# Column stretches of 512 instead of 384 in batches 1 to 3 of an attention and token mixer, with a new order of the work

## The chip, the cores and the metric

The kernel runs on one core of a Trainium2 chip. TensorE (PE) multiplies, with its weight loads shown apart as PEld; VectorE (DVE), ScalarE (ACT) and GpSimd (POOL) work element by element; SyncE (SP) issues the transfers. The metric is the device time of one execution in microseconds, the median of several runs. The runs of the kernel before have a median of 217.35 us and a lowest time of 216.99 us.

## The reference, cut to what matters

For 4 batches of 1088 tokens a linear attention is computed, four heads of 32 columns each, whose features are the 64 products of two 8-wide projections of a query or a key:

```python
a = einsum('rd,bhsd->bhsr', S1, x); b = einsum('rd,bhsd->bhsr', S2, x)
phi(x) = outer(a, b)                         # 64 features
x = (phi(q) @ (phi(k)^T v)) / (phi(q) @ sum(phi(k)) + 1e-6)   # B x 1088 x 128
h = relu(x^T @ w_tok1) @ w_tok2              # over tokens, 256 wide
u = x + h^T
out = u + relu(u @ w_ch1) @ w_ch2            # over channels, 1536 wide
```

The weights arrive as 64-bit floats; the kernel rebuilds 32-bit floats from them with integer operations.

## The kernel before, in words

A plan of named operations is built, and a list of names, `ORDER` (line 67), says in which order they are issued. Every engine runs its own instructions in that order. A suffix such as `@pool` chooses the engine, and `~4` asks for four filler matmuls. The sets of buffers (`bufs`, line 223) set how far one engine can run ahead of another.

The names: `K1.p` projects the keys of batch 1, `K1.v0`, `v4`, `v8` form their products on DVE, `K1.s` sums them against the values on PE and `K1.kvz` copies the result; `Q1.p` projects queries, `Q1.w`, `Q1.r` write and read them back by DMA and `Q1.m` multiplies. `A1.x` is the attention itself, `A1.n`, `A1.r`, `A1.d` its division, `A1.h` and `A1.l` split the result in a rounded high part and the rest. `A1.t` and `A1.w` are the two token products; `A1.xb` transposes x on DVE, `A1.xm` and `A1.xT` carry it through DRAM, `A1.us` adds it, and `A1.uh`, `A1.ul` split the sum u. `w20.abs` to `w20.add` convert piece 0 of the third weight, `w20.hi` and `w20.lo` split it.

The channel product is cut along the tokens into stretches, `U0` to `U11` (lines 42 to 57). Batch 0 has stretches of 384, 384 and 320 columns. Batches 1 to 3 are laid end to end, and their 3264 columns are cut into seven stretches of 384, one of 320 and one of 256, so that a stretch may hold the end of one batch and the start of the next. For each of the 12 pieces of the 1536 channels of a stretch there are four operations: `U.f`, three matmuls into a bank of `ps_h` (line 928); `U.h`, the rectified high part on ACT (line 932); `U.l`, the rest on DVE (line 935); and `U.s`, three matmuls that add into the bank of `ps_o` that collects the stretch's output (line 941). A high part and its rest stay in one of `HID` = 4 sets until `U.s` has read them. At a stretch's end `U.ol` adds the output to u on DVE (lines 960, 966) and `U.out` stores it (line 977). There are 3 banks of `ps_h`, 2 of `ps_o` and 3 of `ps_a`; `K0.s` sums into a bank of `ps_o`, `K1.s` to `K3.s` into one of `ps_a` (line 477).

The loads are issued by SP in the order of `LOADS` (line 36) for batches 0 and 1 and the weights, and where `ORDER` names them for batches 2 and 3.

Of the kernel before, what the change touches and what calls it, by code (L numbers as in the profile page):

```python
# [10 lines left out]
F32R = mybir.dt.float32r  # L11
# [49 lines left out]
HID = 4  # L61
# [9 lines left out]
v0 ~2 K0.s00 K0.s04 Q0.a10 K0.v8 K0.s08 Q0.m10 w01.shift w01.merge d04 d03 Q0.a11 Q0.b11 Q0.m11 w04.abs
w04.clamp@dve w03.abs w03.clamp@dve Q0.p2 Q0.a20 Q0.m20 Q0.a21 Q0.b21 w03.shift w04.shift d13 d10 Q0.m21 w03.merge
d12 K0.s10 K0.s14 K0.s18 w01.add d11 d20 K0.kvz ~2 A0.x0 w03.low q1 A0.n0 w10.abs A0.x1 A0.n1 k1 w04.merge A0.r0
A0.d0 d30 w04.low w04.add A0.r1 d31 w10.clamp@dve A0.d1 A0.x2 A0.t0 A0.n2 A0.t1 A0.r2 w03.add w10.shift A0.d2 Q1.p
w12.abs w11.abs w12.low v1 w20.abs w10.merge w12.clamp@dve w11.clamp@dve d21 d15 w10.low Q1.c0 w10.add Q1.c1 w11.low
# [10 lines left out]
w14.merge w15.low U0.h U0.s w15.add U0.h U0.l w01.hi U0.l U0.f w00.hi U0.h U0.l w02.hi U0.f U1.f w14.add w00.lo@dve
U0.h w10.hi U0.s A0.w2 U1.h U1.l U0.s K1.kvz A0.uh22 U0.l U1.f w15.hi U0.oh@pool U1.h U0.s Q1.r0None Q1.r00 Q1.r01
Q1.r1None Q1.r10 Q1.r11 Q1.m00@dve Q1.m11@pool U0.s U1.s U1.f U1.h Q1.m01@pool U1.f U1.l w03.lo@pool U1.s U1.oh@pool
w13.hi U1.f U0.ol Q1.m10@dve U0.out A0.ul22 w13.lo@pool w02.lo@pool A1.x w01.lo@pool U1.l U1.h U1.l w14.hi q2
w10.lo@pool U1.f U1.h U1.l U1.s U1.s w04.lo@pool U1.s A1.n0 U2.f U2.f k2 v2 A1.r0 A1.d0 q3 A1.n2 A1.r2 U1.h A1.n1  # L90
# [30 lines left out]
U9.s U9.h U10.f U9.l U10.f U9.l U10.h U9.s U10.f U10.h U9.s U10.h U9.s U10.l U10.l U10.s U10.f U10.f U10.s U9.ol
U9.out U10.h U10.h U10.l U10.s U10.l U10.f U10.f U10.s U10.h U10.h U10.l U10.f U10.s U10.h U10.l U10.s U10.f U10.h
U10.l U10.f U10.s U10.h U10.l U10.f U10.h U10.l U10.l U10.f U10.s U10.l U11.f U10.s U10.s U10.h U10.l U11.f U10.s
U11.f U11.h U11.h U11.h U11.l U11.l U10.s U11.s U11.f U11.f U11.s U10.ol U10.out U11.l U11.h U11.h U11.f U11.h U11.s
# [928 lines left out]
```

## Time and profile before

| what | value |
|---|---|
| median of the runs | 217.35 us |
| lowest run | 216.99 us |
| the profiled execution, its own time | 216.37 us |
| its span, first to last instruction | 213.9 us |
| PE busy | 209.5 us, 98% |
| PEld busy | 199.1 us, 93% |
| DVE busy | 147.1 us, 69% |
| ACT busy | 116.2 us, 54% |
| POOL busy | 60.9 us, 28% |
| DMA, mean over the span | 133 GB/s |

Busy time of PE overstates its use, since matmuls overlap and their ends are modelled. The chain of waits, which counts each stretch of time once, gives what a matmul really costs in a stream: the time of a piece divided by its matmuls. A timeline row gives the start, the length, the engine, the line and the shapes of one group of instructions.

### The profile page before, as it was taken

The numbers are of one execution on the slowest core, as the hardware profiler recorded it, in microseconds if no ns is written. First come the engines' busy times: TensorE is split into PE (matmuls) and PEld (weight loads), VectorE is DVE, ScalarE is ACT, GpSimd is POOL, SyncE is SP. The second block draws the span as 40 slices with busy tenths as digits, with TensorE's granted clock in tenths as the row PEclk, the third lists the DMA queues.
The fourth block names the chain that finished last, engine by engine and source line by source line (L and its number), as shares of the span: only waits on it lengthen the run. The fifth ranks groups of instructions, "written<-read, shape, count | busy, mean of one in ns | idle before, by whom it ended". The sixth has DMA issues, their size and how long they took to land.

```text
span 213.9 us, 4865 instructions
## 1 busy us (share of the span) xinstructions
PE 209.5 (98%) x1876; PEld 199.1 (93%) x1876; DVE 147.1 (69%) x299; ACT 116.2 (54%) x282; POOL 60.9 (28%) x66
## 2 busy tenths in 40 slices
PE   8999999999999999999999999999999999999993
PEld 7779779999998999999999999999999999999993
DVE  2899999998789765777434666585547656556562
ACT  4788997988456245444344544443336453544541
POOL 3177686989971001301000660010000010000000
PEclk9999999999999999999999999999999999999999
DMA  6999985750778598300697400014400200100000
GB/s 223 402 405 409 399 328 129 138 146 10 241 304 242 148 193 171 135 3 3 203 221 184 123 29 0 3 37 142 120 0 0 78 0 0 37 3 37 0 31 25
DMA packets 11398, 28.35 MB, mean 133 GB/s; under 512 B 1520, under 2 KB 5616, under 8 KB 11376
## 3 DMA queue, kind: packets, MB, share of 16 engines
q1 hardware_dynamic: 11232, 27.79, 41.7%
q8 instruction: 14, 0.23, 0.5%
q10 hardware_dynamic: 144, 0.26, 0.5%
q14 instruction: 8, 0.07, 0.1%
HBM read 23.21 MB, written 4.83 MB: 131 GB/s over the span
## 4 chain that ended last, share of the span: by engine, by line
PE 97%; ACT 1%; DVE 0%; issue 0%
PE ps_o L941 34%; PE ps_h L928 33%; PE ps_a L758 5%; PE ps_a L692 4%; PE ps_a L878 4%; PE ps_o L264 3%; PE ps_a L483 3%; PE ps_a L436 2%; PE ps_a L874 2%; PE ps_a L752 1%; PE ps_a L574 1%; PE ps_o L483 1%; PE ps_a L629 1%; PE ps_h L574 1%; PE ps_a L783 1%; PE ps_a L792 1%
## 5 line engine op out<-in xcount | busy, mean ns | idle before, releaser
L935 DVE SCALAR_TENSOR_TENSOR hl<-ps_h,hh 128x384 fp32r<-128x384 f32 (+2 forms) x144 | 74.5, 531 | 46.0 <-ACT hh L932 45.3
L932 ACT ACTIVATE hh<-ps_h 128x384 fp32r<-128x384 f32 (+2 forms) x144 | 67.4, 474 | 63.1 <-PE ps_h L928 54.0
L928 PE MATMUL ps_h<-uh,halves 128*128 128x384 f32 (+2 forms) x288 | 85.4, 330 | 0.0
L941 PE MATMUL ps_o<-hh,halves 128*128 128x384 f32 (+2 forms) x288 | 71.2, 330 | 0.0
L928 PEld LDWEIGHTS ps_h<-uh,halves 128*128 128x128 f32 x288 | 53.1, 188 | 0.6
L941 PEld LDWEIGHTS ps_o<-hh,halves 128*128 128x128 f32 x288 | 50.2, 188 | 0.8 <-issue 0.4
L928 PE MATMUL ps_h<-ul,halves 128*128 128x384 f32 (+2 forms) x144 | 47.1, 327 | 0.0
L941 PE MATMUL ps_o<-hl,halves 128*128 128x384 f32 (+2 forms) x144 | 47.1, 327 | 0.0
L852 POOL TENSOR_TENSOR ul<-us,uh 128x320 fp32r<-128x320 f32 (+4 forms) x10 | 7.2, 727 | 71.1 <-ACT uh L849 71.1
L928 PEld LDWEIGHTS ps_h<-ul,halves 128*128 128x128 f32 x144 | 27.1, 188 | 0.2 <-DVE ul L852 0.2
L941 PEld LDWEIGHTS ps_o<-hl,halves 128*128 128x128 f32 x144 | 27.1, 188 | 0.0
L307 POOL TENSOR_TENSOR whole<-c,tail 128x512 int32<-128x512 int32 (+3 forms) x11 | 11.7, 1072 | 2.7 <-ACT tail L290 1.3
L286 ACT ACTIVATE c<-doubles 128x512 f32<-128x512 f32 (+3 forms) x17 | 10.5, 625 | 3.1 <-DMA doubles<-wt 2.5
L466 DVE TENSOR_TENSOR k_p<-ps_a,a_sb 128x1024 f32<-128x1024 f32 (+1 forms) x12 | 11.0, 947 | 0.0
L722 POOL TENSOR_TENSOR xl<-x,xh 128x384 fp32r<-128x384 f32 x3 | 3.0, 1014 | 26.0 <-ACT xh L718 26.0
L290 ACT ACTIVATE tail<-doubles 128x512 int32<-128x512 uint32 (+3 forms) x17 | 10.4, 625 | 0.0
L300 DVE SCALAR_TENSOR_TENSOR c<-doubles,ps_h 128x512 int32<-128x512 int32 (+3 forms) x17 | 10.3, 609 | 0.2
L297 DVE TENSOR_SCALAR ps_h<-c 128x512 int32<-128x512 int32 (+3 forms) x17 | 10.2, 613 | 0.1
L758 PE MATMUL ps_a<-halves,xh 128*128 128x256 f32 x54 | 9.8, 283 | 0.0
L692 PEld LDWEIGHTS ps_a<-kvz,qp 128*64 128x64 f32 x288 | 8.7, 138 | 0.9 <-issue 0.7
L692 PE MATMUL ps_a<-kvz,qp 128*64 128x66 f32 x288 | 9.3, 223 | 0.0
L264 PE MATMUL ps_o<-still 128*128 128x128 f32 x38 | 8.0, 364 | 1.1 <-DVE still L242 1.1
(85 smaller groups left out, 238.7 us busy)
## 6 DMA issues: line engine op xcount, KB each, us to landing
qp<-rows SPq DMA_DIRECT2D x6, 544.0 KB, 5.0
br<-rows SPq DMA_DIRECT2D x12, 272.0 KB
doubles<-wc SPq DMA_DIRECT2D x6, 512.0 KB, 5.9
v_sb<-v SPq DMA_DIRECT2D x4, 594.0 KB, 10.6
doubles<-wt SPq DMA_DIRECT2D x4, 512.0 KB, 5.4
k_sb<-kT SPq DMA_DIRECT2D x3, 576.0 KB
xm<-xb SPq DMA_DIRECT2D x3, 576.0 KB
xT<-xm SPq DMA_DIRECT2D x12, 144.0 KB, 3.2
```

The costliest lines, as they stand in the source:

```text
L264: nc.tensor.matmul(spare_ps[:, :P], lhsT=still, rhs=still, start=True, stop=True)
L286: nc.scalar.activation(f32(t["c"]), f32(high), AF.Abs)
L290: nc.scalar.activation(t["tail"], low.bitcast(U32), AF.Copy, scale=2.0 ** -29)
L300: nc.vector.scalar_tensor_tensor(t["c"], high, -(1 << 30), t["ps"], op0=ALU.bitwise_and, op1=ALU.bitwise_or)
L307: engines[e].tensor_tensor(dst(), t["c"], t["tail"], op=ALU.add)
L466: engines["pool" if on_pool else "dve"].tensor_tensor(t["k_p"][:pn, t0 * H:t1 * H], a.unsqueeze(3).broadcast_to([pn, n, R, R]), t["sb", t0 ...
L692: nc.tensor.matmul(x_ps[c:c + 64, o:o + 2 * (D + 1)], lhsT=qp[:, p, s0 + c:s0 + c + 64], rhs=kvz_all[b % 2][:, p, :2 * (D + 1)], start=Tru ...
L758: nc.tensor.matmul(t["h_ps"][:, :DTOK], lhsT=t[l][:m, i, :], rhs=part(0, piece, r, j * DTOK, DTOK)[:m], start=(i == 0 and k == 0), stop=(i ...
L928: nc.tensor.matmul(h_ps[:, :cn], lhsT=part(2, at[2][e][0], l, at[2][e][1] * P, P), rhs=r[:, :cn], start=(m == 0), stop=(m == 2))
L932: nc.scalar.activation(t["hh"][:, :cn], t["h"][:, :cn], AF.Relu)
L935: nc.vector.scalar_tensor_tensor(t["hl"][:, :cn], t["h"][:, :cn], 0.0, f32(t["hh"][:, :cn]), op0=ALU.max, op1=ALU.subtract)
L941: nc.tensor.matmul(outs[i][:, :cn], lhsT=part(3, at[3][e][0], l, at[3][e][1] * P, P), rhs=r[:, :cn], start=(e == 0 and m == 0), stop=(e == ...
```

## The change: what it does

The stretches of batches 1 to 3 become five of 512 columns, one of 448 and one of 256, so that there are ten stretches, `U0` to `U9`, instead of twelve. The sets for the high part and its rest grow to 512 columns, and there are 3 instead of 4; those of u (`u`, `uh`, `ul`) go from 4 to 3. In the last stretch every fourth channel piece uses the buffers `xh` and `xl` of the attention result instead. `K2.s` and `K3.s` sum into a bank of `ps_o`. The loads of queries, keys and values of batches 2 and 3 are issued as two transfers of 64 partitions each, and so is the store of `U3`. `LOADS` and `ORDER` are written anew.

```diff
-LOADS = "00 q0a 02 k0 q0b 01 v0 04 03 13 10 12 11 20 q1 k1 30 31 v1 21 15 14 32 22".split()
-WIDE = 384
+LOADS = "00 q0a 02 k0 q0b 01 03 v0 04 10 12 20 11 13 q1 30 k1 31 21 v1 32 22 15 14".split()
+WIDE = 512
...
-    for n in (384,) * 7 + (320, 256):
+    for n in (512,) * 5 + (448, 256):
...
-HID = 4
+HID = 3
+HALVED = {"q2", "k2", "v2", "q3", "k3", "v3"}
 ORDER = """
...
+U3.s U4.f U4.h U4.h U3.ol U4.l U4.l U4.f U4.h A2.t2 U4.f U4.s U4.s U4.f U4.h A2.relu A2.hT A2.hTh U4.l U4.l U4.f
...
-    bufs = {..., "u": 4, "uh": 4, "ul": 4, ...
+    bufs = {..., "u": 3, "uh": 3, "ul": 3, ...
...
     def load(name, dst, src, nbytes, after=(), takes=(), uses=(), boost=0.0):
+        cuts = (0, P // 2, P) if name in HALVED else (0, P)
         def emit(_):
-            nc.sync.dma_start(dst(), src)
+            t = dst()
+            for p0, p1 in zip(cuts, cuts[1:]):
+                nc.sync.dma_start(t[p0:p1], src[p0:p1])
...
-                    t["kv"] = bank("ps_a" if b else "ps_o")
+                    t["kv"] = bank("ps_a" if b == 1 else "ps_o")
...
+                lent = i == len(SPANS) - 1 and e % 4 == 3
-                ps, hid = Hold("ps_h"), Hold("hid")
+                ps, hid = Hold("ps_h"), Hold("xs" if lent else "hid")
...
+                    if lent:
+                        t["hh"], t["hl"] = (new(x, [P, NT, P], F32R).rearrange("p t c -> p (t c)") for x in ("xh", "xl"))
...
+                    cuts = (0, P // 2, P) if i == 3 else (0, P)
+                        for p0, p1 in zip(cuts, cuts[1:]):
+                            nc.sync.dma_start(out[b][p0:p1, c0:c0 + m], outs["sb", i][p0:p1, d0:d0 + m])
```

Three places show how the order moves. The first is PE in the start, from the second query projection to the attention of batch 0. Rows with `still` are fillers, `s_spread` is `Q0.p`, `k_p` is `K0.s`, and `kvz` is `A0.x`. Before:

```order
L264 MATMUL ps_o<-still 128x128 x3
L574 MATMUL ps_a<-q_sb,s_spread 128x384 x2
L574 MATMUL ps_h<-q_sb,s_spread 128x384 x2
L264 MATMUL ps_o<-still 128x128 x2
L483 MATMUL ps_o<-v_sb,k_p 64x66 x18
L574 MATMUL ps_a<-q_sb,s_spread 128x320 x2
L574 MATMUL ps_h<-q_sb,s_spread 128x320 x2
L483 MATMUL ps_o<-v_sb,k_p 64x66 x18
L264 MATMUL ps_o<-still 128x128 x2
L692 MATMUL ps_a<-kvz_84,qp 64x66 x36
```

and now:

```order
L261 MATMUL ps_o<-still 128x128 x2
L575 MATMUL ps_a<-q_sb,s_spread 128x384 x2
L575 MATMUL ps_h<-q_sb,s_spread 128x384 x2
L261 MATMUL ps_o<-still 128x128 x4
L575 MATMUL ps_a<-q_sb,s_spread 128x320 x2
L575 MATMUL ps_h<-q_sb,s_spread 128x320 x2
L484 MATMUL ps_o<-v_sb,k_p 64x66 x36
L261 MATMUL ps_o<-still 128x128 x2
L693 MATMUL ps_a<-kvz_84,qp 64x66 x36
```

One filler fewer stands ahead of the second query projection and two more behind it, and the key sums stand behind the third projection in one piece.

The second place is DVE around the transposition of batch 2's attention result. `rec` and `x` are the division, `xb` the transposition, `xl` and `ul` splits, and `hl` is `U.l`. Before:

```order
L935 SCALAR_TENSOR_TENSOR hl<-ps_h,hh 128x384 x3
L704 RECIPROCAL rec<-den 128x12 x2
L712 TENSOR_TENSOR x<-ps_a,rec 128x384 x2
L704 RECIPROCAL rec<-den 128x12
L712 TENSOR_TENSOR x<-ps_a,rec 128x384
L812 STREAM_TRANSPOSE xb<-x 128x1152
L935 SCALAR_TENSOR_TENSOR hl<-ps_h,hh 128x384
```

and now:

```order
L940 SCALAR_TENSOR_TENSOR hl<-ps_h,hh 128x512
L723 TENSOR_TENSOR xl<-x,xh 128x384
L713 TENSOR_TENSOR x<-ps_a,rec 128x384
L853 TENSOR_TENSOR ul<-us,uh 128x256
L705 RECIPROCAL rec<-den 128x12
L713 TENSOR_TENSOR x<-ps_a,rec 128x384
L813 STREAM_TRANSPOSE xb<-x 128x1152
L940 SCALAR_TENSOR_TENSOR hl<-ps_h,hh 128x512
```

One division moved ahead of the `U.l` above it, and two splits came into the piece of the row that has no `U.l`.

The third place is PE around the key sums of batch 3, `K3.s`. `uh` rows are `U.f`, `hh` and `hl` rows `U.s`, `s_rows` is `Q3.p`. Before:

```order
L928 MATMUL ps_h<-uh,halves_500 128x384
L483 MATMUL ps_a<-v_sb,k_p 64x66 x36
L629 MATMUL ps_a<-q_sb,s_rows 32x272 x8
L941 MATMUL ps_o<-hh,halves_790 128x384 x2
L941 MATMUL ps_o<-hl,halves_790 128x384
```

and now:

```order
L946 MATMUL ps_o<-hh,halves_674 128x512 x2
L946 MATMUL ps_o<-hl,halves_674 128x512
L484 MATMUL ps_o<-v_sb,k_p 64x66 x36
L693 MATMUL ps_a<-kvz_84,qp 64x66 x36
L930 MATMUL ps_h<-uh,halves_653 128x512
```

The sums now go into a bank of `ps_o` in the middle of stretch `U3`, directly ahead of batch 2's attention; the next user of that pool, the first `U4.s`, takes the bank of `U3` and so comes behind `U3.ol`, as the line of `ORDER` in the diff has it.

## Rows read from the trace of the kernel before

**Rows 1.** The page's parts 1 and 2: busy time of each engine, and the span in 40 slices, the busy share of PE in tenths and the granted clock in tenths of full speed.

```profile
PE 209.5 (98%) x1876; PEld 199.1 (93%) x1876; DVE 147.1 (69%) x299; ACT 116.2 (54%) x282; POOL 60.9 (28%) x66
...
PE   8999999999999999999999999999999999999993
...
PEclk9999999999999999999999999999999999999999
```

**Rows 2.** The chain of waits in the start, in order of time: start us, length us, what.

```profile
11.12 0.65 PE ps_h L574 x4
11.77 0.64 PE ps_o L264 x4
12.41 1.20 PE ps_o L483 x36
13.61 0.74 PE ps_a L574 x4
14.35 0.54 PE ps_h L574 x4
14.89 1.20 PE ps_o L483 x36
16.09 0.64 PE ps_o L264 x4
16.73 2.25 PE ps_a L692 x72
18.98 2.79 PE ps_a L752 x12
21.77 0.73 PE ps_a L629 x16
...
24.38 0.44 PE ps_a L792 x2
```

**Rows 3.** The chain of waits later on, the same columns: pieces of 384, 320 and 256 columns, and the end.

```profile
179.11 2.08 PE ps_o L941 x12
...
193.34 0.88 PE ps_h L928 x6
...
206.03 1.06 PE ps_o L941 x9
...
209.21 1.43 PE ps_o L941 x12
210.63 0.02 issue
210.66 0.42 DVE o_sb L966
```

**Rows 4.** Groups of instructions by line and shape, on DVE: busy us and mean ns of one, then idle time before them.

```profile
L935 DVE SCALAR_TENSOR_TENSOR hl<-ps_h,hh 128x384 fp32r<-128x384 f32 x108 | 58.4, 553 | 37.2 <-ACT hh L932 36.5
...
L935 DVE SCALAR_TENSOR_TENSOR hl<-ps_h,hh 128x256 fp32r<-128x256 f32 x12 | 4.9, 424 | 3.1 <-ACT hh L932 3.1
...
L812 DVE STREAM_TRANSPOSE xb<-x 128x1152 f32<-128x1152 f32 x3 | 4.1, 1380 | 0.1
```

**Rows 5.** The same view on ACT.

```profile
L932 ACT ACTIVATE hh<-ps_h 128x384 fp32r<-128x384 f32 x108 | 52.4, 492 | 49.6 <-PE ps_h L928 43.0 <-PE ps_o L941 6.0
...
L932 ACT ACTIVATE hh<-ps_h 128x256 fp32r<-128x256 f32 x12 | 4.5, 383 | 4.4 <-PE ps_h L928 3.8 <-PE ps_o L941 0.6
```

**Rows 6.** Timeline of SP's issues: start us, length us; the first two are the issue of weight piece 20 and of `q1`, the others the first and last `Q1.r` and the store of `U0` with the four loads behind it.

```profile
10.52 0.33 SPq L268 DMA_DIRECT2D doubles<-wc  x1
12.03 0.33 SPq L268 DMA_DIRECT2D q_sb<-qT  x1
...
33.08 0.63 SPq L659 DMA_DIRECT2D qp<-rows  x1
...
35.78 1.28 SPq L662 DMA_DIRECT2D br<-rows  x2
53.93 0.36 SPq L977 DMA_DIRECT2D outT<-o_sb  x1
54.34 0.43 SPq L268 DMA_DIRECT2D q_sb<-qT  x1
```

**Rows 7.** The page's part 2 again, what the DMA moved in GB/s in each of the 40 slices, and from part 6 the reads of `Q.r`, KB each and us to landing.

```profile
GB/s 223 402 405 409 399 328 129 138 146 10 241 304 242 148 193 171 135 3 3 203 221 184 123 29 0 3 37 142 120 0 0 78 0 0 37 3 37 0 31 25
...
qp<-rows SPq DMA_DIRECT2D x6, 544.0 KB, 5.0
```

**Rows 8.** Timeline of POOL, the first two products `Q1.m`.

```profile
50.41 3.64 POOL L672 TENSOR_TENSOR qp<-qp,br 128x544 f32<-128x544 f32 x2
```

**Rows 9.** Timeline of DVE around the division and transposition of batch 2: start us, length us, what, and idle time before it.

```profile
95.45 1.08 DVE L935 SCALAR_TENSOR_TENSOR hl<-ps_h,hh 128x384 fp32r<-128x384 f32 x2 [0.19 <-ACT hh L932]
98.02 0.32 DVE L704 RECIPROCAL rec<-den 128x12 f32<-128x12 f32 x2 [1.49 <-ACT den L700]
98.38 1.02 DVE L712 TENSOR_TENSOR x<-ps_a,rec 128x384 f32<-128x384 f32 x2
...
100.16 1.38 DVE L812 STREAM_TRANSPOSE xb<-x 128x1152 f32<-128x1152 f32 x1
101.47 0.52 DVE L935 SCALAR_TENSOR_TENSOR hl<-ps_h,hh 128x384 fp32r<-128x384 f32 x1
```

More of the change, by code (lines that the diff above doesn't have):

```diff
@@ L71 @@
[L71 to L75, printed above, removed]
@@ L86 @@
[L86 to L90, printed above, removed]
@@ L121 @@
[L121 to L124, printed above, removed]
-U11.l U11.f U11.l U11.f U11.s U11.s U11.l U11.s U11.f U11.h U11.h U11.l U11.f U11.s U11.l U11.f U11.s U11.h U11.h
@@ L126 @@
-U11.l U11.l U11.f U11.s U11.h U11.h U11.s U11.l U11.l U11.s U11.s U11.ol U11.out
+s k0a d00 s.abs s.clamp s.shift s.merge s.low s.add ~4 K0.p0 s.rows q0a w00.abs w00.clamp@dve K0.c0 K0.v0 w00.low
+w00.shift d02 k0 Q0.s0@pool Q0.s1@pool ~1 Q0.p0 w02.abs Q0.a00 ~1 K0.p4 w02.clamp@dve Q0.b01 w00.merge w00.add
+Q0.m00 Q0.a01 Q0.m01 K0.c8 q0b ~2 Q0.p1 K0.c4 d01 w02.low w02.shift K0.v8 w02.merge w02.add w01.abs K0.v4 Q0.a10
+Q0.m10 w01.clamp@dve w01.shift Q0.b11 Q0.a11 Q0.m11 d03 w03.abs w01.low ~4 Q0.p2 v0 K0.s00 K0.s04 d04 w03.clamp@dve
@@ new lines @@
+Q0.a20 w01.merge w01.add w04.abs w04.clamp@dve Q0.m20 w04.low Q0.a21 Q0.b21 Q0.m21 d10 w10.abs K0.s08 K0.s10 K0.s14
+K0.s18 K0.kvz ~2 A0.x0 w03.shift w10.low A0.n0 w04.shift w03.merge w04.merge w04.add d12 w12.abs d20 d11
+w10.clamp@dve A0.r0 A0.d0 w12.clamp@dve A0.x1 A0.n1 A0.r1 d13 w10.shift A0.d1 A0.x2 A0.t0 A0.t1 w03.low w03.add q1
+w12.low A0.n2 A0.r2 w20.low w10.merge w10.add A0.d2 Q1.p w13.abs w11.abs w12.shift w11.clamp@dve w13.clamp@dve
+w20.abs w11.shift w20.clamp@dve w12.merge w11.merge w12.add Q1.c0 Q1.c1 d30 w13.low w11.low k1 A0.t2 w11.add
@@ new lines @@
+w20.shift A0.relu ~2 A0.hT K1.p d31 d21 w13.shift w20.merge w20.add v1 w30.abs d32 w30.clamp@dve Q1.w0 A0.hTh
+w13.merge w13.add d22 K1.c0 K1.v0 w30.shift w30.merge A0.u0 A0.w0 A0.u1 A0.w1 K1.c4 w30.low w02.hi K1.c8 w20.hi
+w20.lo@pool A0.uh00 A0.ul00 U0.f U0.f Q1.w3 w21.abs K1.v4 U0.f w31.abs K1.v8 d15 Q1.w1 w31.clamp@dve K1.s
+w21.clamp@dve A0.uh11 U0.h A0.ul11 w30.add w30.hi w30.lo@pool U0.h w22.abs w31.low U0.h w22.clamp@pool w21.low U0.l
+U0.l U0.s w21.shift U0.l w21.merge w21.add w31.shift w31.merge w31.add w32.abs w32.low w12.hi w32.clamp@dve U1.f
@@ new lines @@
+U1.h U0.s U1.f U1.h A0.u2 U0.s w21.hi w21.lo@pool w15.low U1.f U1.h d14 Q1.w2 w22.low q2 U1.l U1.l w31.hi U1.s
+w22.shift U1.l w31.lo@pool w22.merge U0.f U0.h w22.add K1.kvz U0.l U1.s U1.s U0.f U0.f U0.s U1.f w14.abs
+w14.clamp@dve U0.h w15.abs U0.h U0.l U0.l w15.clamp@pool U0.s U1.h U1.l U1.f U0.s w22.hi w32.shift U1.f U1.h U1.h
+w10.hi U1.l w32.merge w22.lo@pool U1.l w15.shift w15.merge w32.add U1.s U1.s U0.f U0.f w15.add w11.hi w14.low U0.h
+U0.l U0.h U1.s w32.hi w32.lo@pool U0.f U0.h U0.l U0.s U0.s w14.shift U0.l w14.merge U0.f Q1.r0None U0.f U0.f U0.h
@@ new lines @@
+U7.s U8.h U8.l U8.s U8.f U8.h U8.l U8.s U8.h U8.l U7.ol U8.f U8.h U8.l U8.f U8.f U8.h U8.l U8.s U8.h U8.s U8.f U8.l
+U8.h U8.l U8.s U8.f U8.h U8.f U8.f U8.l U8.s U8.h U8.s U8.s U8.h U8.l U8.f U8.f U8.h U8.s U8.l U8.l U8.s U8.s U8.h
+U8.l U9.f U9.h U9.l U9.f U8.s U9.h U9.l U9.f U9.h U9.f U9.h U8.ol U8.out U9.f U9.l U9.l U9.s U9.s U9.s U9.f U9.h
+U9.h U9.f U9.s U9.l U9.s U9.f U9.l U9.f U9.s U9.h U9.l U9.s U9.f U9.h U9.h U9.l U9.l U9.f U9.s U7.out U9.f U9.h U9.h
+U9.l U9.l U9.h U9.l U9.s U9.s U9.s U9.s U7.out U9.ol U9.out
@@ L266, in load @@
     def load(name, dst, src, nbytes, after=(), takes=(), uses=(), boost=0.0):
+        cuts = (0, P // 2, P) if name in HALVED else (0, P)
         def emit(_):
-            nc.sync.dma_start(dst(), src)
-        op = plan.add(name, {"sp": 475.0}, emit, (), takes, uses, boost, order=after)
+            t = dst()
+            for p0, p1 in zip(cuts, cuts[1:]):
+                nc.sync.dma_start(t[p0:p1], src[p0:p1])
+        op = plan.add(name, {"sp": 475.0 * (len(cuts) - 1)}, emit, (), takes, uses, boost, order=after)
         op.bytes, op.rate = nbytes, 395.0
@@ L498, in keys @@
         n = f"K{b}"
-        kp_hold, kv_hold = Hold("k_p"), Hold("ps_a" if b else "ps_o")
+        kp_hold, kv_hold = Hold("k_p"), Hold("ps_a" if b == 1 else "ps_o")
         sb = {i: Hold("a_sb") for i in (0, 4, 8)}
```

82 lines of the change are left out of this document (34 added, 48 removed).

## The prediction

> **What bounds the kernel now.** I read the page's shares first, then the chain of waits from the start to the end, then groups by shape, and last the issues of SP. PE is busy 98% of the span and in every slice but the first and the last, at full granted clock throughout [rows 1]. Busy time alone would not prove that PE is the bound, because overlapping matmuls are counted in full; the chain does. From 24.38 us, the transposes of batch 0's token product, the chain runs on PE without a break to the last matmul, whose piece ends 1.43 us after 209.21 [rows 2, 3], and the page's chain names no other engine there. What follows is one addition of 0.42 us and the last store. In the start the chain runs on PE too, but part of what it runs there is filler (two pieces of 0.64 us in [rows 2]).
>
> So three things can move the end: how long PE's own work takes after 24.38 us, when that point comes, and any wait that the new order puts into a stream that has none.
>
> What a matmul costs in the stream is read from the pieces of the chain. Twelve of 384 columns take 2.08 us, which is 173.3 ns each; six of 320 take 0.88 us, 146.7 ns each; nine of 256 take 1.06 us, 117.8 ns each [rows 3]. From 320 to 384 columns that is 26.6 ns for 64 columns, 0.416 ns a column, and what stays beside the columns is 173.3 - 384 x 0.4167 = 13.3 ns at 384, 13.3 ns at 320 and 11.1 ns at 256.
>
> **The change part by part.**
>
> *Wider stretches.* Each stretch has 12 x 6 = 72 matmuls whatever its width. Before, batches 1 to 3 take 7 x 72 at 173.3, 72 at 146.7 and 72 at 117.8 ns: 87.3 + 10.6 + 8.5 = 106.4 us. After, 5 x 72 = 360 are of 512 columns, 72 of 448 and 72 of 256. No row has 512 or 448 columns. With the fixed 13.3 ns a matmul of 512 takes 226.7 ns and one of 448 takes 200.0 ns: 81.6 + 14.4 + 8.5 = 104.5 us. That is **1.9 us less**, the fixed part of the 144 matmuls that disappear. The bounds: if the part beside the columns grows in proportion, 512 costs 173.3 x 512 / 384 = 231.1 ns and 448 costs 202.2, in all 106.2 us, and the gain is 0.2 us; if it is the smallest that the rows show, 11.1 ns, the sum is 360 x 224.4 + 72 x 197.8 + 72 x 117.8 = 103.5 us, and the gain is 2.9 us. I take 13.3 ns, because the two nearest widths, 384 and 320, both show it.
>
> [...]
>
> *DVE and ACT.* `U.l` costs 553 ns at 384 columns and 424 at 256 [rows 4], about 1.0 ns a column, so 682 ns at 512; `U.h` costs 492 and 383 [rows 5], so 600 ns at 512. A channel piece of 512 columns gives PE 6 x 226.7 = 1.36 us of work, so both keep up, with more room than now (553 of 1.04 us). Their saved fixed parts are worth nothing, since PE covers them.
>
> *The start.* Ahead of the second query projection one filler goes (two fillers, four rows of the trace, take 0.64 us, so 0.32), behind it two are added (0.64), and the key sums come in one piece behind the third projection [rows 2]. Counted on from the row at 16.73, the attention of batch 0 starts 0.3 us later, at 17.05, and with it all that hangs on it, to the point at 24.38. Is something else later? Weight piece 03 now goes ahead of `v0`. In the rows SP issues piece 20 at 10.52 and `q1` at 12.03 [rows 6], with gaps before them that I read as waits for the landing of the eighth transfer before; for `q1`, the sixteenth, that is `v0`, so `v0` lands at about 12.0. Piece 03 is 512 KB, at 402 to 409 GB/s [rows 7] 1.3 us, so `v0` lands at 13.3. PE reaches the key sums at 12.41 - 0.32 + 0.64 + 1.28 = 14.0. It is covered by 0.7 us. Behind it the weights of the first token product and `q1` have the same bytes ahead of them. I take **+0.3 us**; the bounds are 0 (if the fillers only fill a wait, as they are meant to) and +1.0 (if the 0.7 us of cover is gone and as much again is lost).
>
> *SP.* The halves add six issues of loads and one of a store, about 0.4 us each [rows 6], on a queue that stands idle for long. `q2` is now ahead of the `Q1.r` reads, 544 KB or about 1.4 us at the rate of [rows 7]. Those reads were issued from 33.08, the last pair over 1.28 us from 35.78, and take 5.0 us to land [rows 6, 7], so until about 42; their first products start at 50.41 [rows 8]. Eight microseconds cover the 1.4. The other loads of batch 2 no longer stand behind the store of `U0` at 53.93 [rows 6], which only makes them earlier. Nothing waits for either on PE, so I cost both at nothing. The new store order at the end leaves the last stretch at 256 columns with the same addition of 0.42 us, so the end costs what it did.
>
> *Banks and sets.* `K3.s` now takes one of two output banks inside stretch `U3`, so the first `U4.s` waits for `U3.ol`, an addition of 512 columns (about 0.7 us, like `U.l`) behind `U3`'s last `U.s`. The order puts two `U4.f`, the last third of `A2.t` and a third `U4.f` between: 3 x 0.68 + 9 x 117.8 ns = 3.1 us of PE work. Covered. Without that cover it would cost 0.7 us and the hand-overs. With three sets instead of four, the time that DVE may be late shrinks: a set is held for `U.h`, `U.l` and `U.s`, at 384 columns 0.49 + 0.55 + 0.52 = 1.56 us, and four sets give 4 x 1.04 = 4.16, so 2.6 us to spare; at 512 it is 0.60 + 0.68 + 0.68 = 1.96 of 3 x 1.36 = 4.08, so 2.1; at 384 with three sets 3.12 - 1.56 = 1.6. I cost this at 0, between a gain of 0 (no wait exists to remove) and the loss of the second rival.
>
> **The sum:** -1.9 + 0.3 = -1.6 us. The span goes from 213.9 to 212.3 us, the profiled execution from 216.37 to 214.8. The median of the runs is 217.35, 1.0 us above the profiled one; I predict the median, 217.35 - 1.6 = **215.8 us**.
>
> **The rivals.**
>
> 1. *No gain from width.* What stands beside the columns grows with them, as it does from 256 to 320 (11.1 to 13.3 ns), and 512 columns cost 231.1 ns. Then 217.35 - 0.2 + 0.3 = 217.5 us. Against it: 320 and 384 show the same 13.3 ns. [...] Chance 0.14 for both.
>
> 2. *Slower: DVE is late for `U.s`.* DVE has stretches without a `U.l` in each of batches 1 to 3. In the row before, `U.l` ends at 96.53 and the next starts at 101.47 [rows 9]; its own work there is three divisions and the transposition, 3 x 0.5 + 1.38 = 2.9 us. Where such a stretch is longer than the time to spare, PE stands still for the rest. With 2.1 us to spare that is 0.8 us for batches 2 and 3, with 1.6 in stretch `U1` 1.3 us for batch 1; the splits that now stand in batch 2's piece add about 1.0. In all 0.8 + 0.8 + 1.3 + 1.0 = 3.9 us, so 217.35 - 1.6 + 3.9 = 219.7 us. It decides the sign from 1.6 us of such waits on. Against it: in [rows 9] nearly 5 us pass without a `U.l` and the chain still has no break, because PE runs the attention, key sums and token products meanwhile, and the new order has them there too. Chance 0.20 for 217.9 to 221.7; over that, 0.05 more, which takes some of the same in the converting of the weights, where DVE has no idle time to lend.
>
> 3. *More gain.* The start is not later and the fixed part is 11.1 ns or the fillers yield: 217.35 - 2.9 = 214.4, and as much as 1 us below that if the first weights, now loaded in another order, let the point at 24.38 come earlier. For it: PE holds filler in the start. Against it: the key sums cannot start before their products, which the same DVE row delivers. Chance 0.11, of which 0.03 lies below 213.0.
>
> That the change would not do what it says can be left out: the order has the 512-column rows.
>
> **How the numbers follow.** The forecast has the remaining 0.50, from about 214.9 to 217.0, since waits of up to 1 us in a new order are likely somewhere. The range must hold 8 in 10: forecast, rival 1, rival 3 down to 213.9 and the lower part of rival 2 up to 218.6, together about 0.82. Two per cent of 217.35, about what a measurement of this kernel can tell from no change, is 4.3 us: faster means below 213.0 (0.03), slower above 221.7 (0.05), and the rest, 0.92, is within.
>
> **What would show it.** In the changed kernel's chain a `U.f` or `U.s` of three 512-column matmuls should take 0.68 us; 0.69 or more is rival 1. The transposes of batch 0 should start at 24.4 to 24.9. The chain from there on should name PE alone; pieces of DVE (`hl`) or ACT (`hh`) in it, and PE rows with idle time put down to them, are rival 2, first to be looked for behind `A1.x`, `A2.x` and `A3.x` and at the first `U4.s`. The forecast is wrong if the clock granted is not full throughout, or if PE waits for `v0`.

## The result and the profile after

On the same chip the changed kernel has a median of 218.35 us (216.13 to 220.41, 15 runs) and the kernel before one of 216.24 us. The ratio is 1.0066, with a 95% interval of 1.0036 to 1.0095: **0.7% slower**. That is within 2%, but of the other sign. 218.35 us lies inside the range, 2.5 us above the number I gave; but on this chip the kernel before took 1.1 us less than the 217.35 us that I had counted from, and the ratio put on 217.35 gives 218.8 us, just above the range. The comparisons leave disturbed runs out.

The page of the changed kernel, parts 1 and 2, answers to [rows 1] and [rows 7]; the DMA row is the busy share of the DMA engines in tenths, the last row GB/s.

```profile
span 216.8 us, 4522 instructions
PE 209.5 (97%) x1734; PEld 183.2 (84%) x1734; DVE 142.4 (66%) x267; ACT 112.0 (52%) x257; POOL 68.8 (32%) x71
PE   8998999999599999999999999999999999999994
PEclk9999999999799999999999999999999999999999
DMA  6999996998406699530697200034010010000020
GB/s 218 376 409 404 409 365 163 156 169 178 133 4 181 192 221 199 150 92 8 189 276 191 54 0 0 3 157 109 0 48 3 0 51 0 0 3 0 0 91 24
```

142 matmuls fewer, and PE as busy as before. One slice has a hole, the eleventh, 54.2 to 59.6 us; the clock is lower in the same slice; and in the three slices ahead of it the DMA engines are busy eight tenths of the time or more and move 156 to 178 GB/s. Neither the hole nor the lower clock is in [rows 1].

The chain of waits of the changed kernel, in the start, around the hole, and later (start us, length us, what):

```profile
16.96 1.72 PE ps_a L693 x53
18.68 0.57 issue
19.24 0.80 PE ps_a L693 x19
...
37.80 16.94 DMA br<-rows
...
54.86 0.20 DVE qp L673
...
55.82 1.52 DVE qp L673
...
57.38 3.58 PE ps_a L693 x68
...
160.34 2.06 PE ps_h L930 x9
...
200.24 1.80 PE ps_o L946 x9
...
212.44 1.37 PE ps_o L946 x12
...
213.84 0.42 DVE o_sb L971
```

A chain that ran on PE alone from 24.38 us on now leaves it: the matmuls of `A1.x` wait for a product `Q1.m` on DVE, and that waits for a read of `Q1.r`, issued at 37.2 and landed 16.94 us after 37.80, at 54.74. The timeline of PE there has the hole itself (start us, length us, what, idle time before it):

```profile
54.80 0.34 PE L693 MATMUL ps_a<-kvz,qp 128*64 128x66 f32 x4
57.38 3.58 PE L693 MATMUL ps_a<-kvz,qp 128*64 128x66 f32 x68 [2.25 <-DVE qp L673]
60.90 0.44 PE L930 MATMUL ps_h<-uh,halves 128*128 128x384 f32 x1
```

Four of the 72 matmuls run, PE stands 2.25 us, and the other 68 take 3.58 us, where all 72 took 2.25 before, as the chain of the kernel before has it:

```profile
55.85 2.25 PE ps_a L692 x72
```

From there to the last matmul the chain has no break again.

The changed kernel by stretches: start, end and length in us, the busy us of PE, PEld, DVE, ACT and POOL, each with its instructions in brackets, then the granted clock, the busy share of the DMA engines and GB/s.

```profile
38.00:42.00 4.00, 4.00 (x25) 4.00 (x24) 3.21 (x7) 3.94 (x11) 3.82 (x4) 1.00 0.87 156
42.00:46.00 4.00, 4.00 (x25) 3.97 (x24) 3.76 (x8) 3.34 (x8) 3.85 (x4) 1.00 1.05 156
46.00:50.00 4.00, 4.00 (x25) 4.00 (x25) 3.83 (x8) 2.86 (x7) 3.52 (x4) 1.00 1.00 180
50.00:54.00 4.00, 4.00 (x22) 3.68 (x22) 1.30 (x3) 2.90 (x8) 1.76 (x2) 1.00 0.90 182
54.00:58.00 4.00, 1.75 (x21) 1.36 (x22) 3.14 (x3) 1.53 (x4) 3.97 (x3) 0.87 0.51 153
58.00:62.00 4.00, 4.00 (x68) 3.93 (x67) 3.90 (x9) 0.54 (x3) 0.46 (x1) 0.71 0.11 39
```

From 38 to 54 us the DMA engines are busy 0.87 of the time or more, and they move less than half of the 402 to 409 GB/s of the start [rows 7]. Behind the hole the granted clock is 0.71 in a stretch of 4 us; by single microseconds it is 0.50 from 57 to 60 us. And this is what SP issued ahead of the hole, its timeline:

```profile
29.62 1.22 SPq L269 DMA_DIRECT2D q_sb<-qT  x2
34.52 0.58 SPq L660 DMA_DIRECT2D qp<-rows  x1
...
37.18 1.20 SPq L663 DMA_DIRECT2D br<-rows  x2
38.47 1.17 SPq L269 DMA_DIRECT2D k_sb<-kT  x2
39.74 3.97 SPq L269 DMA_DIRECT2D v_sb<-v  x2
46.75 3.51 SPq L269 DMA_DIRECT2D q_sb<-qT  x2
```

`q2` stands ahead of the reads of `Q1.r` and `k2`, `v2`, `q3` right behind them, each in two pieces of 64 partitions; before, all four came behind the store of `U0`, from 54.34 us on [rows 6].

**Where the time went**, from the two traces. The transposes of `A0` start at 25.46 instead of 24.38 us, +1.1. From there to the last addition it is 188.4 us instead of 186.3, +2.1. In those 2.1 the matmuls of `A1.x` end at 60.96 where they would have ended at 54.80 + 2.25 = 57.05, +3.9, and the rest is 1.8 us shorter. Behind the last addition it is 0.3 us shorter. In all +2.9, from a span of 213.9 to one of 216.8.

### The profile page after: what moved, and what is told of

It is laid out like the page before. It is cut to its first block, busy times and chain, and to the rows that moved or that the text cites. A ratio compares the mean times of both kernels' runs of the same rounds, so it can differ in the third digit from the quotient of the medians.

```text
span 216.8 us, 4522 instructions
## 1 busy us (share of the span) xinstructions
PE 209.5 (97%) x1734; PEld 183.2 (84%) x1734; DVE 142.4 (66%) x267; ACT 112.0 (52%) x257; POOL 68.8 (32%) x71
## 4 chain that ended last, share of the span: by engine, by line
PE 79%; DMA 13%; POOL 3%; SPq 1%; issue 1%; DVE 1%; ACT 1%; DVEq 0%
PE ps_o L946 28%; PE ps_h L930 28%; DMA br<-rows 8%; PE ps_a L693 5%; PE ps_a L759 4%; PE ps_a L879 4%; PE ps_o L484 3%; DMA k_sb<-kT 3%; DMA rows<-abT 2%; PE ps_a L437 1%; PE ps_a L753 1%; POOL c L310 1%; PE ps_o L261 1%; PE ps_a L630 1%; POOL c L294 1%
## 5 line engine op out<-in xcount | busy, mean ns | idle before, releaser
L940 DVE SCALAR_TENSOR_TENSOR hl<-ps_h,hh 128x512 fp32r<-128x512 f32 (+4 forms) x117 | 70.3, 613 | 46.7 <-ACT hh L937 45.0
L937 ACT ACTIVATE hh<-ps_h 128x512 fp32r<-128x512 f32 (+4 forms) x117 | 62.2, 539 | 62.7 <-PE ps_h L930 36.4
L930 PE MATMUL ps_h<-uh,halves 128*128 128x512 f32 (+4 forms) x240 | 78.5, 362 | 0.0
L946 PE MATMUL ps_o<-hh,halves 128*128 128x512 f32 (+4 forms) x234 | 65.4, 362 | 0.0
L930 PEld LDWEIGHTS ps_h<-uh,halves 128*128 128x128 f32 x240 | 44.3, 188 | 5.6 <-DVE hl L940 0.3
L946 PEld LDWEIGHTS ps_o<-hh,halves 128*128 128x128 f32 x234 | 41.6, 188 | 5.3 <-issue 0.4
L930 PE MATMUL ps_h<-ul,halves 128*128 128x512 f32 (+4 forms) x120 | 42.9, 358 | 0.0
L946 PE MATMUL ps_o<-hl,halves 128*128 128x512 f32 (+4 forms) x117 | 42.2, 361 | 0.0
L673 POOL TENSOR_TENSOR qp<-qp,br 128x544 f32<-128x544 f32 x9 | 12.1, 1367 | 27.0 <-DMA br<-rows 27.0
L410 POOL TENSOR_TENSOR halves<-whole,halves 128x512 fp32r<-128x512 f32 (+3 forms) x9 | 9.8, 1103 | 3.8 <-ACT halves L407 3.8
L301 DVE SCALAR_TENSOR_TENSOR c<-doubles,ps_h 128x512 int32<-128x512 int32 (+3 forms) x17 | 10.1, 606 | 0.1
```

The lines of the kernel that those rows point to most:

```text
L673: engines[e].tensor_tensor(qp[:, p, cs], qp[:, p, cs], t["br"][:, p, cs], op=ALU.mult)
L930: nc.tensor.matmul(h_ps[:, :cn], lhsT=part(2, at[2][e][0], l, at[2][e][1] * P, P), rhs=r[:, :cn], start=(m == 0), stop=(m == 2))
L937: nc.scalar.activation(t["hh"][:, :cn], t["h"][:, :cn], AF.Relu)
L940: nc.vector.scalar_tensor_tensor(t["hl"][:, :cn], t["h"][:, :cn], 0.0, f32(t["hh"][:, :cn]), op0=ALU.max, op1=ALU.subtract)
L946: nc.tensor.matmul(outs[i][:, :cn], lhsT=part(3, at[3][e][0], l, at[3][e][1] * P, P), rhs=r[:, :cn], start=(e == 0 and m == 0), stop=(e == ...
```

## The experiments

Three things are new at the hole: loads ahead of the reads, loads behind them, and the shape of the loads. Theory A of the first runs is that the loads, moved from behind `U0`'s store to around the reads, delay them. The rivals are in each expectation. Where a diff of `ORDER` is shown, only the words around the moved name stand there.

**1. `q2` behind the reads** (`k2`, `v2`, `q3` follow it on SP).

```diff
-Q1.w2 w22.low q2 U1.l U1.l
+Q1.w2 w22.low U1.l U1.l
...
-Q1.m00@pool Q1.r10 Q1.r11 Q1.m10@dve
+Q1.m00@pool Q1.r10 Q1.r11 q2 Q1.m10@dve
```

> The changed kernel with one load moved: the queries of batch 2 (q2) are issued behind the reads of Q1.r instead of ahead of them. Theory A (the reads are delayed by whatever shares the DMA engines with them, and by the loads ahead of them most): the last read lands some 2 us earlier, at about 52 to 53 instead of 54.7, the first attention matmuls of batch 1 still wait a little, span 214 to 216 us instead of 216.8. Theory B (only bytes ahead in the queue delay the reads): the last read lands by 51, no wait at the attention, span 212.5 to 213. Theory C (the reads are slow by themselves): landing unchanged, span 216.8.

Measured: 216.08 us, ratio 0.9957 (0.9909 to 1.0004), under the interval of the change. The profiled execution took 722 us and is no use as a trace, so where the reads landed is not known. The other nine lie in two groups, five from 214.79 to 215.24 and four from 216.92 to 218.81; the times of run 5, whose trace has no hole, lie in two groups too (214.67 to 215.27 and 216.44 to 216.50), so the groups do not tell a hole from none. So `q2` is a part of it, but its place alone doesn't settle it.

**2 and 3. Loads held until the reads have landed.** A tiny transfer, `mark`, which reads the tile that `Q1.r` fills, is put on SP behind the reads, so that SP issues nothing more until they have landed. In `hold_k2` this holds `k2`, `v2` and `q3`, in `hold_all` `q2` too, which also moves behind it. The loads are halved as in the change.

```diff
+        if b == 1:
+            def hold_back(_):
+                nc.sync.dma_start(dram.tile([2, 2, 8], F32, name="mark"), t["br"][63:65, :, :8])
+            plan.add(f"{n}.gate", {"sp": 650.0}, hold_back, reads[0] + reads[1], (), [br_hold], boost)
...
-Q1.m00@pool Q1.r10 Q1.r11 Q1.m10@dve
+Q1.m00@pool Q1.r10 Q1.r11 Q1.gate Q1.m10@dve
```

> The changed kernel with q2 still ahead of the Q1.r reads, but k2, v2 and q3 held back on SP by a transfer of a few bytes that reads what Q1.r brings, so that they start only when the reads have landed. Theory A (loads behind the reads take DMA time from them): the last read lands at 48 to 51 instead of 54.7, PE does not wait at batch 1's attention, the granted clock stays full, span 212 to 213.5 us. Theory B (only bytes ahead count): landing and span as in the changed kernel, 54.7 and 216.8. Theory C: as B.

> The changed kernel with q2, k2, v2 and q3 all held back until the Q1.r reads have landed, as the wait for U0's store held them back in the kernel before. Theories A and B: the reads land by 48 to 49 (in the kernel before the DMA moved their 2.2 MB at 130 to 145 GB/s until about 48), PE has no wait at batch 1's attention, full clock, span 212 to 213 us, so 1 to 2 us under the kernel before. Theory C: span 216.8.

Measured: 214.74 us, ratio 0.9895 (0.9844 to 0.9945), and 214.70 us, ratio 0.9885 (0.9825 to 0.9945). In `hold_all` `mark` goes out at 49.23, which is when the reads have landed, and `q2`, the next load, at 49.95. `A1.x` runs whole; the chain of `hold_all`:

```profile
54.43 2.25 PE ps_a L697 x72
56.68 0.72 PE ps_h L934 x3
```

So the loads make the hole, and without it the change is faster than the kernel before. `hold_k2` does as well with `q2` ahead of the reads: what hurts is what runs beside them.

**4. The kernel before with the loads in the new places**, whole.

```diff
-A1.x w01.lo@pool U1.l U1.h U1.l w14.hi q2 w10.lo@pool
+A1.x w01.lo@pool U1.l U1.h U1.l w14.hi w10.lo@pool
...
-U0.s Q1.r0None Q1.r00 Q1.r01 Q1.r1None Q1.r10 Q1.r11 Q1.m00@dve
+U0.s q2 Q1.r0None Q1.r00 Q1.r01 Q1.r1None Q1.r10 Q1.r11 k2 v2 q3 Q1.m00@dve
...
-A1.n0 U2.f U2.f k2 v2 A1.r0 A1.d0 q3 A1.n2
+A1.n0 U2.f U2.f A1.r0 A1.d0 A1.n2
```

> The kernel before with the changed kernel's issue order on SP alone: q2 ahead of the Q1.r reads, k2, v2 and q3 directly behind them, no longer behind the store of U0. Theory A: the reads land at 53 to 55 instead of about 48, batch 1's attention, due at 55.7 here, waits for their products up to 3 us, and with a fall of the clock the span grows from 213.9 to 215.5 to 218 us. Theory B: 214 to 215. Theory C (the supply order is not the cause): 213.9.

Measured: 216.83 us, ratio 1.0015 (0.9976 to 1.0053); the span is 213.9 us, as before. The reads do land later: POOL's first product starts at 52.28 instead of 50.41 us [rows 8], behind 1.70 us of waiting for them. But `A1.x` starts at 55.96 and runs whole, 2.27 us for its 72 matmuls in the chain. The same loads at the same place cost nothing here, so place was not enough. What this kernel lacks is the halves, and in 38 to 50 us it moves 185 to 207 GB/s at the share of DMA time at which the changed kernel moves 156 to 180. That gave theory H: the halves do it.

**5. The changed kernel with whole loads.**

```diff
-HALVED = {"q2", "k2", "v2", "q3", "k3", "v3"}
+HALVED = set()
```

> The changed kernel with every late load in one piece of 128 partitions instead of two of 64; order as in the changed kernel, so q2 still stands ahead of Q1.r's reads and k2, v2, q3 right behind them. Theory H (the halves make the collision: in the kernel before with the same order and whole loads the DMA engines moved 185 to 207 GB/s at full busy share, in the changed kernel 156 to 182): the reads of Q1.r land by about 51 instead of 54.7, A1.x runs without a break, span about 213.0, time 0.98 to 0.99 of the kernel before. Rival A (the place of the loads alone is the cause, whatever their shape): the reads land at about 54, A1.x is broken as in the changed kernel (2 us or more on DVE's qp), span 216 or more.

Measured: 214.97 us, ratio 0.9939 (0.9903 to 0.9976), span 213.0. Theory H holds, a little short of its numbers (0.98 to 0.99, and reads by about 51). By stretches, `whole_loads` beside the rows of the changed kernel above:

```profile
38.00:42.00 4.00, 4.00 (x25) 4.00 (x24) 3.23 (x7) 3.94 (x11) 3.81 (x4) 1.00 1.00 182
42.00:46.00 4.00, 4.00 (x25) 3.98 (x24) 3.73 (x9) 3.31 (x9) 3.83 (x4) 1.00 1.00 209
46.00:50.00 4.00, 4.00 (x25) 4.00 (x24) 3.86 (x8) 2.86 (x7) 3.52 (x4) 1.00 1.07 198
50.00:54.00 4.00, 4.00 (x23) 3.68 (x22) 3.28 (x7) 2.90 (x8) 1.72 (x3) 1.00 0.54 173
```

The loads stand at the same places in the order, and the DMA engines are again full, but they move 182 to 209 GB/s and are done earlier, with a share of 0.54 in the last row where the changed kernel has 0.90. PE is busy throughout and the clock stays at 1.00. DVE's timeline in `whole_loads` has the last products `Q1.m`, with 0.41 us of waiting for a read:

```profile
51.93 1.36 DVE L673 TENSOR_TENSOR qp<-qp,br 128x544 f32<-128x544 f32 x2 [0.41 <-DMA br<-rows]
```

The reads landed at 51.9 instead of 54.7 us, and `A1.x` runs whole, as the chain of `whole_loads` has it:

```profile
54.78 2.25 PE ps_a L693 x72
```

Of the 2.8 us between the two landings 1.2 are there before the reads start: SP issues the last pair at 35.94 us here and at 37.18 in the changed kernel. So the halved `q2`, which stands ahead of them, also makes the reads go out later.

**6. The kernel of run 4 with the halves**, the same question from the other side.

```diff
+HALVED = {"q2", "k2", "v2", "q3", "k3", "v3"}
...
+        cuts = (0, P // 2, P) if name in HALVED else (0, P)
         def emit(_):
-            nc.sync.dma_start(dst(), src)
+            t = dst()
+            for p0, p1 in zip(cuts, cuts[1:]):
+                nc.sync.dma_start(t[p0:p1], src[p0:p1])
```

> The kernel before with q2 ahead of Q1.r's reads, k2, v2 and q3 right behind them (as in the run before_early), and now those loads in halves of 64 partitions. Theory H: the reads land later than in before_early, where POOL waited 1.7 us for them: POOL's wait grows to 4 us or more, A1.x at about 56 breaks, and the time is 1.01 or more of the kernel before. Rival A (shape of the loads has no part): as before_early, no break, span about 213.9, ratio 1.00.

Measured: 217.82 us, ratio 1.0065 (1.0034 to 1.0096), span 215.9: the same ratio as the change, in a kernel with 384 columns, four sets and the old order of everything else. The timeline of POOL, and then of PE, in this kernel:

```profile
55.55 2.63 POOL L677 TENSOR_TENSOR qp<-qp,br 128x544 f32<-128x544 f32 x2 [5.02 <-DMA br<-rows]
```

```profile
55.85 0.34 PE L697 MATMUL ps_a<-kvz,qp 128*64 128x66 f32 x4
58.23 2.20 PE L697 MATMUL ps_a<-kvz,qp 128*64 128x66 f32 x68 [2.05 <-POOL qp L677]
```

POOL waits 5.0 us where it waited 1.7 in run 4, and `A1.x` is broken; only the ratio stays under the 1.01 that I expected. The last reads are issued 1.8 us later than in run 4, at 37.66 instead of 35.90. So the halves need neither the new width nor the new order to do their damage.

**7. Is it two transfers for one, or pieces of 64 partitions?** The changed kernel with the loads cut by columns, 128 partitions a piece.

```diff
-        cuts = (0, P // 2, P) if name in HALVED else (0, P)
+        wide = src.shape[1]
+        cuts = (0, wide // 2, wide) if name in HALVED else (0, wide)
...
-            for p0, p1 in zip(cuts, cuts[1:]):
-                nc.sync.dma_start(t[p0:p1], src[p0:p1])
+            for c0, c1 in zip(cuts, cuts[1:]):
+                nc.sync.dma_start(t[:, c0:c1], src[:, c0:c1])
```

> The changed kernel with its late loads still in two pieces, but cut by columns (128 partitions, half the columns each) instead of by partitions (64 partitions, all the columns). Theory P (the pieces of 64 partitions are what is slow): it behaves as whole_loads, reads of Q1.r landed by about 51, A1.x unbroken, span about 213.0, and SP issues v2 and q3 without the 3.5 to 4 us they took in the changed kernel. Theory N (two transfers in place of one are what is slow, whatever their shape): as the changed kernel, reads at about 54.7, A1.x broken by 2 us or more, span 216 or more.

Measured: 214.84 us, ratio 0.9903 (0.9863 to 0.9943), span 212.0. The chain of `col_halves`:

```profile
53.94 2.25 PE ps_a L694 x72
```

It behaves as with whole loads: from 38 to 50 us it moves 178 to 217 GB/s, and DVE's last products start at 51.27. So it is the 64 partitions. One thing I expected is missing: SP still took 2.47 us for `v2` and 2.48 for `q3`, where the whole ones took 0.38 and 0.57. Here the long issues go with the pieces, whatever their cut; but behind the mark in `hold_all` two halves took only 1.18 and 1.24. Nothing waited for them.

**8. What the halves cost by themselves.** `hold_all` with whole loads, so that the four loads run alone behind the mark in both kernels.

```diff
-HALVED = {"q2", "k2", "v2", "q3", "k3", "v3"}
+HALVED = set()
```

> hold_all (q2, k2, v2 and q3 held back until Q1.r's reads have landed) with these loads whole instead of halved. If halved loads cost DMA time of their own, the four loads behind the mark, issued at about 49 to 54 us, take fewer microseconds at a high DMA share than in hold_all, whose DMA share there the trace has. For the time both theories say the same as hold_all and whole_loads, 214.7 to 215.0 us, 0.985 to 0.995 of the kernel before, with A1.x unbroken; a version 0.5 us or more under those two would show that something of the collision was left in whole_loads.

Measured: 214.90 us, ratio 0.9918 (0.9883 to 0.9952), no better than whole loads left where they stood, so nothing shows that some of the collision is left in `whole_loads`. By stretches, first `hold_all` (64 partitions a piece), then `hold_whole`:

```profile
50.00:52.00 2.00, 2.00 (x13) 1.76 (x11) 1.69 (x4) 1.18 (x3) 1.31 (x1) 1.00 0.34 78
52.00:54.00 2.00, 2.00 (x13) 1.92 (x12) 1.83 (x4) 2.00 (x6) 0.41 (x1) 1.00 1.07 258
54.00:56.00 2.00, 2.00 (x59) 1.75 (x59) 1.40 (x4) 1.28 (x5) 2.00 (x3) 1.00 1.00 238
56.00:58.00 2.00, 2.00 (x32) 1.93 (x29) 1.90 (x7) 0.99 (x4) 1.22 (x2) 1.00 1.03 233
58.00:60.00 2.00, 2.00 (x14) 1.75 (x14) 1.61 (x5) 0.90 (x3) 1.85 (x2) 1.00 1.03 232
60.00:62.00 2.00, 2.00 (x41) 1.93 (x42) 2.00 (x3) 2.00 (x7) 0.08 (x1) 1.00 0.57 130
```

```profile
50.00:52.00 2.00, 2.00 (x13) 1.76 (x11) 1.69 (x4) 1.21 (x3) 1.29 (x1) 1.00 0.62 194
52.00:54.00 2.00, 2.00 (x13) 1.92 (x12) 1.84 (x4) 2.00 (x6) 0.43 (x1) 1.00 0.99 364
54.00:56.00 2.00, 2.00 (x59) 1.75 (x59) 1.39 (x4) 1.26 (x5) 2.00 (x3) 1.00 1.00 402
56.00:58.00 2.00, 2.00 (x32) 1.93 (x27) 1.90 (x7) 1.00 (x4) 1.22 (x2) 1.00 0.52 208
```

Both move the same: 2 us times the sum of the rates is 2.34 MB in each. The shares times 2 us add up to 10.1 us of full DMA with the pieces and 6.3 us without, 3.8 us more. Pieces of 64 partitions run at 232 to 258 GB/s, whole loads at 364 to 402.

**9 and 10. The start.** The chain puts the break of 0.57 us in `A0.x` down to no engine. I took it to come from `Q0.m21` on POOL, which now stands behind the addition of weight piece 01. `pool_order` puts that addition behind `Q0.m21`; `both` does this and holds the loads as `hold_all`.

```diff
-Q0.a20 w01.merge w01.add w04.abs w04.clamp@dve Q0.m20 w04.low Q0.a21 Q0.b21 Q0.m21 d10
+Q0.a20 w01.merge w04.abs w04.clamp@dve Q0.m20 w04.low Q0.a21 Q0.b21 Q0.m21 w01.add d10
```

> The changed kernel with the add of weight piece 01 put behind Q0.m21 on POOL; nothing else moved. If the 0.57 us break inside A0.x comes from Q0.m21 standing behind that add, the break is gone, A0.x runs in 2.25 us without it and hT comes 0.5 to 0.8 us earlier than 25.46. Theory A/H on the loads says that the time hardly gains from it: Q1.r's reads are issued and land no earlier, so that A1.x waits as much longer as the start is earlier, and the span stays at 216 to 216.8. Rival (the start carries through to the end): span 0.5 to 0.8 us shorter, about 216.1.

> The changed kernel with all four late loads held back until Q1.r's reads have landed (as in hold_all) and the add of piece 01 behind Q0.m21 on POOL. With no break at A1.x the earlier start should carry to the end: hT at about 24.7, span 212.3 to 212.7 (hold_all 213.1), time 0.98 to 0.99 of the kernel before. Rival: A1.x waits for the reads instead (they land at about 50, its matmuls would come half a microsecond earlier than 54.4), and the span stays at 213.0.

Measured: 218.04 us, ratio 1.0028 (0.9984 to 1.0073), and 216.25 us, ratio 0.9974 (0.9945 to 1.0002). Both miss. The break is gone, but so it is in the traces of `hold_all`, `col_halves` and `hold_whole`, where the addition has its early place. And the transposes of `A0` start at 26.28 and 27.05 us, later and not earlier (the first is from an execution of 219.60 us, so the second counts). In the chain of `both`

```profile
23.42 1.00 POOL whole L307
...
24.45 0.81 ACT c L286
25.26 0.56 ACT abT L638 x2
25.82 0.77 ACT tail L290 x2
```

ACT converts weights behind an addition that POOL starts at 23.42 us, and at 21.27 in `hold_all`. That putting off piece 01 put off this one is likely and not shown. By the medians, from two chips, `hold_all` is 1.6 us faster. What makes the break stays open.

**The kernels side by side**, us in the trace of each: start of the transposes of `A0`, start of `A1.x`, last addition, and the third less the first.

| kernel | `A0.hT` | `A1.x` | last addition | between |
|---|---|---|---|---|
| before | 24.38 | 55.85 | 210.66 | 186.3 |
| run 4, loads early, whole | 24.60 | 55.96 | 210.65 | 186.1 |
| run 6, loads early, halved | 24.58 | 55.85, broken | 212.82 | 188.2 |
| the change | 25.46 | 54.80, broken | 213.84 | 188.4 |
| `hold_k2` | 25.35 | 54.76 | 209.86 | 184.5 |
| `hold_all` | 24.94 | 54.43 | 210.02 | 185.1 |
| `whole_loads` | 25.39 | 54.78 | 209.90 | 184.5 |
| `col_halves` | 24.45 | 53.94 | 209.06 | 184.6 |
| `hold_whole` | 24.90 | 54.41 | 209.54 | 184.6 |

The last column leaves the start out; each row is one trace. The change without the damage is 1.2 to 1.8 us shorter than before; the halves add 2.1 us in the old kernel and 3.9 in the new. The 1.2 is that of `hold_all`, and there the chain leaves PE once more, for DVE from 79.12 to 83.06 us: two splits `A1.ul` take 1.70 us in it, the `U.l` behind them are late for `U.s`, and PE loses about 0.5 us. In the other traces of the table from `hold_k2` on this is missing, and the gain is 1.7 to 1.8.

Five versions lie under the kernel before with their whole interval, by 0.6 to 1.2%: `hold_k2`, `hold_all`, `whole_loads`, `col_halves` and `hold_whole`. The change lay above it with its whole interval; it was not run beside them on their chips. `whole_loads` is the change with one line undone.

## Why the prediction was wrong

- **The step that failed is *SP*:** "The halves add six issues of loads and one of a store, about 0.4 us each", and in the end "I cost both at nothing". I priced a halved load by its issue on SP. Its price is DMA time: 10.1 us for four loads instead of 6.3, and this at a place where the DMA was needed. The hole it made cost 3.9 us in the trace, against a gain of 1.8, and that took the sign. The forecast had named a granted clock below full as a sign of being wrong; it came, behind the hole.
- **The cover in the same step was misread.** "so until about 42" and "Eight microseconds cover the 1.4" took the landing of 5.0 us, which is the median of the six `qp` reads of all batches, for all the reads of this one. [Rows 7] said otherwise: the ninth slice, 42.8 to 48.1 us, still has 146 GB/s, and only the tenth has 10. `hold_all`, where nothing runs beside the reads, has them landed by 49.23. So the cover ahead of 50.41 was about 1 to 2 us. That their new place "only makes them earlier" was half of the other loads of batch 2: what is earlier shares the DMA with what is there. Runs 4 and 5 show that this sharing with whole loads still cost nothing at `A1.x`.
- **Wider stretches, -1.9 us: right in kind, a little less by the rows.** Nine matmuls of 512 columns take 2.06 us in the chain of the changed kernel, 229 ns each instead of 226.7; nine of 448 take 1.80, 200 ns as forecast; twelve of 256 take 1.37, 114 ns. In all 360 x 0.229 + 72 x 0.200 + 72 x 0.114 = 105.0 us instead of 106.4, a gain of 1.4. The table has 1.2 to 1.8. What makes up the difference was not traced, but for the 0.5 us of `hold_all`. Three matmuls of 512 take 0.69 us, which I had named as the sign of the first rival: its 231.1 ns and my 226.7 lie equally far from 229. Its gain of 0.2 us does not fit the rows. The chance of 0.14 there is for two cases; no run shows the second, and what the rows give is the 1.4 us.
- **The start, +0.3 us: +1.1 in the profiled execution,** and outside the 24.4 to 24.9 us that I had named. PE did not wait for `v0`, and the waits of SP in the trace of the kernel before bear out what I read from its gaps: 1.2 us for `v_sb` ahead of the issue of `q1`. `A0.x` starts at 16.96 instead of 16.73 us, +0.2, which is near the forecast; but it takes 3.09 us instead of 2.25, and most of that is the break in it. But kernels that are alike up to there have the transposes anywhere from 24.45 to 25.46 us, 0.1 to 1.1 above before. +0.3 is within that, and which of the starts a kernel gets was not settled; runs 9 and 10 show only that this move of an addition is not the way in.
- **Banks and sets at nothing: right in the changed kernel.** From 61 us to the end its chain names PE alone; no `hl` or `hh` stands in it, at the first `U4.s` or anywhere else. `hold_all`, with the same sets, has `hl` in its chain once, for the 0.5 us above.
- **The rivals.** The second, DVE late for `U.s`, has the right sign, and of its mechanism only that 0.5 us shows, in a kernel that had no other loss. The slower case that came was not among them: I had named what could go wrong for PE's operands, and not asked what the moved loads would share the DMA with.
- **The sum without the halves.** `whole_loads`, which has all else, is 1.5 us under the kernel before by medians on one chip (214.97 and 216.50); the sum had said 1.6. That is as near by luck of the start as by working: in the traces the two spans are 0.9 us apart, with a gain of 1.8 behind the transposes and a loss of 1.0 ahead of them.

## What to carry to other kernels

Cut a load by columns and not by partitions: two pieces of 64 partitions took 1.6 times the DMA time of the whole load here, and pieces cut by columns cost the kernel nothing (a ratio of 0.9903, with whole loads 0.9939). When loads are moved earlier, read the DMA's busy share over the whole stretch in which they will run, and take the landing of the reads that they meet from the place where the DMA goes quiet, not from a median over the reads of all batches. Look at the granted clock behind a hole on PE: in the changed kernel's trace, where it fell to 0.50, one of 2.25 us went with a loss of 3.9, in run 6, where it stayed at 1.00, one of 2.05 with 2.1.

## What the runs showed of the hardware that I had not expected

- The clock. In the changed kernel PE stood 2.25 us and the next 68 matmuls took 3.58 us, at a granted clock of 0.50 from 57 to 60 us; in run 6 it stood 2.05 us at the same place, the same 68 took 2.20, and the clock stayed at 1.00. By these two traces 1.4 of the 3.9 us were clock. The other executions of the changed kernel put it lower: with a mean clock of 0.992, as the profiled one has, most spans are 216.6 to 217.0 us, and with 1.00 most are 216.1 to 216.2, some 0.6 apart. So the clock is the smaller part, and the kernel is slower without its fall too. What decides between the two was not tried.
- A busy share near 1.0 says little of bytes: 156 GB/s in the changed kernel (42 to 46 us) and 402 in `hold_whole` (54 to 56 us) both stand beside 1.0 or more.
- DVE's last product `Q1.m` took 1.52 us in the changed kernel, where two took 1.36 in `whole_loads`. That lengthened the hole by some 0.8 us; POOL was at work in it, on an addition of its own, which took 1.48 us instead of 1.01. The `ul` split of 256 columns behind the 0.5 us of `hold_all` is a second case: 1.58 us beside a product that POOL starts at 81.00, and 0.42 in `hold_whole`, where POOL starts it at 82.21. No run tried the two apart.
- Not tried: the `br` reads that came late are themselves transfers to 64 partitions, 272 KB each, in every kernel here; no run cut them otherwise.
